# The last row group of the first norm turned by VectorE's block transposes and transfers within SBUF, in place of TensorE

## The chip, the core and the metric

One core of a Trainium2 chip runs the whole program. The core has a matrix engine (TensorE, PE in the profile; its weight loads are listed apart as PEld), three engines for elementwise work (VectorE or DVE, ScalarE or ACT, GpSimd or POOL), and SyncE (SP), which in this kernel issues nearly all transfers. Each engine works through its own queue in order; semaphores tie the queues together. Matmul results land in PSUM, eight banks of 128 × 512 words; everything else on the chip lies in SBUF (128 partitions) or in DRAM. The metric is the device time of one execution in microseconds, the median over runs.

## The reference, cut to what matters

```python
# x (1,2048,448); 16 heads of 28; mod = silu(c) @ w_mod gives six rows: sa, ca, ga, sb, cb, gb
h = _layernorm(x, axis=-1) * (1 + ca) + sa
qkv = h @ wqkv                       # split in q, k, v of 16 heads
p = softmax(q k^T * 28 ** -0.5)
x = x + ga * ((p v) @ wo)
h = _layernorm(x, axis=-1) * (1 + cb) + sb
x = x + gb * gmlp(h)                 # w_in, gelu, layernorm, w_sp over the rows, w_out
```

The change lies in the first line: the norm of the 2048 rows of x and what brings it into the layout in which the products of the next line take it, features on the partitions.

## The kernel before

**Tiles.** The rows come in NG = 4 groups of 512, each as four tiles of 128 rows (`xg`, `xn`). A group's normed rows have to stand as `hT[g]`: features on the partitions in four chunks (128, 128, 128 and 64 features; the last chunk's 64 are kept twice), 512 rows along the free axis. The products are done in three passes on operands split in a high part (fp32r) and a low part (what is left), so `hT[g]` has seven slots: the high parts of chunks 0 to 2, their low parts in slots 3 to 5, and slot 6 for chunk 3, high part in partitions 0 to 63 and low part in 64 to 127. `STEPS` lists the 11 pairs of slots that a product needs.

**Before the main part.** For a group g, `ln_stat` and `ln_rs` (VectorE and GpSimd) get mean and 1/sd of each row, `ln_norm` (VectorE) writes the normed rows `xn`, and `ln_transpose` (line 173) turns them: 16 transposes of 128 × 128 on TensorE into four PSUM banks `tp`, then per chunk one ScalarE activation that scales and shifts (`hfull`, by the columns ca and sa), one that writes the high part, and one VectorE subtraction for the low part. Line 372 copies 64 columns of `xn` so that the last chunk comes out twice. `ln_next(g)` (line 614) turns group g and, between the chunks, takes the statistics of group g + 1 and then norms it.

What uses `hT[g]` are `v_tile` (128 rows of V, 11 matmuls) and `qk_unit((m,), g)` (128 of the 896 Q and K columns for one group, 11 matmuls). In this text "unit (m, g)" is such a Q/K unit. Behind a unit ScalarE writes its high part into a tile `qh`, VectorE the low part into `ql`, and SP stores both to the DRAM scratch `qk_scr`. `qh` and `ql` have two buffers each, so the third unit in a row takes over the buffer of the first.

**Order.** It is written by hand (the scheduler is off): the loop at line 634 goes over g = 1, 2, 3 and lists v tiles, units (0, g) and (3, g), and pieces of the modulation: `mod_acc` (VectorE products of w_mod with silu(c)), `mod_split` (their high and low part), and `mod_bc` and `mod_col` (a sum over the partitions on TensorE, `pc`, read by VectorE; `mod_col` then sends a row through DRAM into a column, by SP). At g = 3 the early buffers are given up, the head buffers `kst` and `qst` take their place, are cleared (`pads`), and head 0 is loaded from `qk_scr`.

**The ramp.** Behind the loop the units left (line 970) run with the first maxima of the attention between their matmuls: `m_first` issues one product `mt` of 128 queries by 512 keys, and VectorE reduces it to its maximum (`pm`, line 717). Units take one of three PSUM banks there, maxima one of the four others. 80 maxima are done in the ramp, then the main part over 16 heads begins.

The second norm of the kernel already has a group turned in another way: `h2_turn` (line 1079) uses VectorE's transpose of 32 × 32 blocks, `h2_put` and `h2_load` move the blocks through DRAM, `h2_group` scales.

Of the kernel before, what the change touches and what calls it, by code (L numbers as in the profile page):

```python
# [8 lines left out]
F32 = mybir.dt.float32  # L9
F32R = mybir.dt.float32r  # L10
AF = mybir.ActivationFunctionType
# [9 lines left out]
NG = 4  # L21
# [78 lines left out]
def tile_adaln_mha_gmlp(ctx, tc, x, wqkv, wo, w_in, w_spT, b_sp, w_out, cT, w_mod0, w_mod, out):  # L100
# [122 lines left out]
    wv = e2.tile([128, 8, D], F32R, name="wv")  # L223
    ones_r = e2.tile([128, 128], F32R, name="ones_r")
    dve.memset(ones_r.bitcast(F32), 1.0)
    wms, xts, raws = {}, {}, {}


    banks, mode = list(range(7)), [None]
# [20 lines left out]

    def load_x(g, eng):
        xg = e1.tile([128, 4, D], F32, name="xg")
        for t0, t1 in ((0, 1), (1, 2), (2, 4)) if g == 0 else ((0, 4),):
            (act if t1 - t0 == 1 else eng).dma_start(xg[:, t0:t1, :], x[g, :, t0:t1])
        for t in range(4):
            xts[4 * g + t] = xg[:, t, :]
# [103 lines left out]
    def ln_norm(g, ts):  # L360
        mv, rs = mv1[g]
        for t in ts:
            xn = e1.tile([128, 512], F32, name="xn", bufs=4)
            dve.tensor_scalar(
                out=xn[:, :D],
                in0=xts.pop(4 * g + t),
                scalar1=mv[:, t, 0:1],
                scalar2=rs[:, t : t + 1],
                op0=ALU.subtract,
                op1=ALU.mult,  # L370
            )
            act.activation(xn[:, D:], xn[:, 384:D], AF.Copy)
            xn1.setdefault(g, []).append(xn)

    ln_stat(0, (0,))
# [233 lines left out]
    def ln_step(g, t):  # L609
        ln_stat(g, (t,))  # L610
        if t % 2:
            ln_rs(g, t - 1, t + 1)

    def ln_next(g):

        if g + 1 < NG:
            ln_transpose(
                xn1.pop(g), e1, hT[g], cols["ca"], cols["sa"], (act,) * 4, (dve,) * 4, None,
                lambda c: ln_step(g + 1, (0, 2, 1, 3).index(c)),
            )  # L620
            ln_norm(g + 1, range(4))
        else:
            ln_transpose(
                xn1.pop(g), e1, hT[g], cols["ca"], cols["sa"], (act,) * 4, (dve,) * 4, None, lambda c: c == 2 and mod_split(1, pool, e1, "wm", 4)
            )

    ln_next(1)
    load_x(3, sp)
# [5 lines left out]
    for g in range(1, NG):  # L634
        if g == 3:
            early.close()
            stk = att.enter_context(tc.tile_pool(name="stk", bufs=1))
            kq = [[stk.tile([128, S], F32R, name=f"{n}st{i}") for n in "kq"] for i in range(3)]
            kst, qst = [a[0] for a in kq], [a[1] for a in kq]
            npool = att.enter_context(tc.tile_pool(name="npool", bufs=2))  # L640
            late_s = ExitStack()
            late_l = late_s.enter_context(tc.tile_pool(name="late_l", bufs=2))

            def pads(i, eng):

                dve.memset(kst[i][64:128, :].bitcast(F32), 0.0)
                eng.memset(qst[i][64:128, :].bitcast(F32), 0.0)
                pool.memset(kst[i][64:86, :].bitcast(F32), 1.0)

            pads(0, dve)  # L650

            def load_head(h, c0=0, c1=S):
                k, q = kst[h % 3], qst[h % 3]
                if h > 2:
                    sp.dma_start(q[84:86, :].bitcast(F32), q[86:88, :].bitcast(F32))
                for r0, i in ((0, 0), (56, 1), (28, 0)):
                    sp.dma_start(k[r0 : r0 + 28, c0:c1].bitcast(F32), qk_scr[i][D + h * DH : D + (h + 1) * DH, c0:c1])
                for r0, i in ((0, 0), (28, 1), (56, 0)):
                    sp.dma_start(q[r0 : r0 + 28, c0:c1].bitcast(F32), qk_scr[i][h * DH : (h + 1) * DH, c0:c1])

            load_head(0, 0, 1536)
            for m in (0, 3):
                qk_unit((m,), g)
            load_head(0, 1536, S)
        v_tile(4 * g)
        if g == 3:
            mod_split(2, dve, late_l, "acc_l", 2)
        v_tile(4 * g + 1)
        if g == 3:
            pads(1, pool)  # L670
            pads(2, pool)
        if g + 1 < NG:
            ln_next(g + 1)
        for k in range(2):
            v_tile(4 * g + 2 + k)
            if g == 2 and k == 1:
                mod_bc("ga", 1, 0)
                mod_col("sb", 1, 1, 0.0)
            if g == 1 or g == 2 and k == 1:
                mod_acc(g, k if g == 1 else 0)  # L680
        if g < 3:
            for k, m in enumerate((0, 3)):
                qk_unit((m,), g)
                mod_acc(g, 3 - g + k)
            if g == 2:
                mod_acc(g, 3)
    mod_col("cb", 2, 0, 1.0)
    mod_bc("gb", 2, 1)
    late_s.close()
# [277 lines left out]
                    for fn, a in when.pop(e):  # L967
                        fn(*a)

    units = [(m, g) for m in (4, 1, 5, 2, 6) for g in range(NG) if g > 0 or m not in (1, 2)]  # L970
    for i, (m, g) in enumerate(units):
        qk_unit(
            (m,),
            g,
            {j: m_first for j in ((1, 3, 5, 7, 9) if i < 8 else (1, 4, 7, 10))},
            put_off=late.setdefault(2, []) if i == len(units) - 1 else None,
        )

# [701 lines left out]
```

## Time and profile before

| | us |
|---|---|
| median of 3 runs | 1370.16 (1369.8 to 1370.71) |
| the profiled execution | 1370.01 |
| its span, first to last instruction | 1368.2 |
| mean granted TensorE clock | 1.000 |

The profile is one execution, taken by the hardware profiler; times of its rows are counted from the start of the span. A timeline row gives start, length, engine, line and operation, what it writes and reads, how many instructions were merged, and in brackets how long the engine had been idle before it and what ended that. Rows of "SPq" are issues of transfers: the length is how long the issuing engine was taken, not how long the data moved. In 40 slices of the span TensorE stands at 9 of 10 or above in all but the last:

```profile
PE   9999999999999999999999999999999999999998
```

### The profile page before, as it was taken

How to read it: one execution, taken by the hardware profiler on the slowest of the kernel's cores; microseconds unless marked ns; L12 is line 12 of the kernel's file. 1: busy time of each engine (PE TensorE's matmuls, PEld its weight loads, DVE VectorE, ACT ScalarE, POOL GpSimd, SP SyncE). 2: the span in 40 equal slices, each digit the busy share in tenths (PEclk: the TensorE clock that was granted, in tenths of full speed). 3: DMA queues.
4: the chain of work that ended last, by engine and by line, in shares of the span. 5: the costliest groups of instructions: out<-in, count | busy, mean ns of one | idle time of the engine just before them, and what ended most of it. 6: DMA issues, size and time to landing. Idle time of an engine off the chain costs nothing.

```text
span 1368.2 us, 20793 instructions
## 1 busy us (share of the span) xinstructions
PE 1361.4 (100%) x7050; PEld 968.0 (71%) x7050; DVE 1112.8 (81%) x1764; ACT 805.2 (59%) x1475; POOL 361.8 (26%) x371
## 2 busy tenths in 40 slices
PE   9999999999999999999999999999999999999998
PEld 8888665556555555555565554788898888888898
DVE  7898899999999999999999991674467777999752
ACT  6623676777677667766776669555335545555411
POOL 2134434244535264654651002210021000000000
PEclk9999999999999999999999999999999999999999
DMA  8465756777677668777873110578604665787553
GB/s 292 135 173 181 234 151 214 210 219 217 222 200 233 189 215 250 215 220 224 248 217 98 43 44 23 181 222 265 228 31 154 221 201 179 254 291 258 180 163 111
DMA packets 144279, 260.21 MB, mean 190 GB/s; under 512 B 22120, under 2 KB 42986, under 8 KB 141626
## 3 DMA queue, kind: packets, MB, share of 16 engines
q1 hardware_dynamic: 141454, 254.69, 59.6%
q10 hardware_dynamic: 2718, 4.19, 0.8%
q8 instruction: 55, 0.90, 0.3%
q14 instruction: 52, 0.43, 0.1%
HBM read 177.67 MB, written 76.34 MB: 186 GB/s over the span
## 4 chain that ended last, share of the span: by engine, by line
PE 96%; issue 1%; DVE 1%; DMA 1%; POOL 0%; ACTq 0%; DVEq 0%; POOLq 0%; SPq 0%
PE st_ps L744 18%; PE mt L712 17%; PE o_ps L759 16%; PE z_ps L1429 5%; PE acc L1498 5%; PE acc L1497 5%; PE acc L1496 5%; PE z_ps L1199 5%; PE pq L407 5%; PE wo_ps L831 3%; PE pv L389 2%; PE y_ps L1569 2%; PE y_ps L1567 2%; PE y_ps L1568 2%; PE acc L1506 1%
## 5 line engine op out<-in xcount | busy, mean ns | idle before, releaser
L717 DVE TENSOR_REDUCE pm<-mt 128x1 f32<-128x512 f32 x1024 | 627.4, 678 | 8.0 <-PE mt L712 8.0
L748 ACT ACTIVATE P<-st_ps 128x512 f32<-128x512 f32 x1024 | 512.6, 640 | 203.1 <-PE st_ps L744 200.6
L744 PE MATMUL st_ps<-qst,kst 128*128 128x512 f32 x1024 | 409.3, 409 | 0.0
L712 PE MATMUL mt<-kst,qst 128*128 128x512 f32 x1024 | 401.5, 392 | 0.2 <-issue 0.2
L744 PEld LDWEIGHTS st_ps<-qst,kst 128*128 128x128 f32 x1024 | 191.3, 188 | 138.5 <-DVE pm L717 65.0
L759 PE MATMUL o_ps<-P,V 128*32 128x512 f32 x2048 | 240.0, 597 | 0.0
L712 PEld LDWEIGHTS mt<-kst,qst 128*128 128x128 f32 x1024 | 192.5, 188 | 34.8 <-ACT P L748 0.8
L869 POOL TENSOR_TENSOR ws_raw<-ws_raw 128x512 f32<-128x512 f32 x112 | 143.5, 1288 | 144.2 <-DMA ws_raw<-in_w_spT_dram 85.4
L1413 ACT ACTIVATE heapB<-raw_sp 128x512 fp32r<-128x512 f32 x156 | 96.7, 630 | 98.9 <-PE acc L1498 71.4
L759 PEld LDWEIGHTS o_ps<-P,V 128*32 128x32 f32 x2048 | 59.1, 109 | 127.2 <-issue 88.9
L1496 PE MATMUL acc<-heapB,heapA 128*128 128x512 f32 x312 | 121.4, 389 | 0.0
L1498 PE MATMUL acc<-heapB,heapA 128*128 128x512 f32 x312 | 121.4, 389 | 0.0
L765 DVE TENSOR_TENSOR osb<-osb,o_ps 128x512 f32<-128x512 f32 x82 | 56.3, 687 | 64.4 <-PE o_ps L759 62.9
L151 DVE TENSOR_TENSOR heapB<-raw_sp,heapB 128x512 fp32r<-128x512 f32 x112 | 74.5, 686 | 28.1 <-ACT heapB L1413 28.0
L1497 PE MATMUL acc<-heapB,heapA 128*128 128x512 f32 x222 | 86.5, 390 | 0.0
L1496 PEld LDWEIGHTS acc<-heapB,heapA 128*128 128x128 f32 x312 | 58.6, 188 | 12.1
L1498 PEld LDWEIGHTS acc<-heapB,heapA 128*128 128x128 f32 x312 | 58.6, 188 | 12.1
L407 PE MATMUL pq<-heapD,heapD 128*128 128x512 f32 x196 | 61.8, 390 | 0.0
L151 POOL TENSOR_TENSOR ws_raw<-ws_raw 128x512 fp32r<-128x512 f32 x44 | 56.7, 1289 | 3.5
L785 POOL TENSOR_TENSOR osb<-osb,rb 128x512 f32<-128x512 f32 x15 | 19.3, 1287 | 114.8 <-DMA rb<-r_scr 65.2
L1497 PEld LDWEIGHTS acc<-heapB,heapA 128*128 128x128 f32 x222 | 41.7, 188 | 9.0 <-DVE heapB L151 0.3
L1432 ACT ACTIVATE z<-z_ps 128x448 f32<-128x448 f32 x32 | 17.4, 545 | 48.0 <-PE z_ps L1429 48.0
(224 smaller groups left out, 1658.1 us busy)
## 6 DMA issues: line engine op xcount, KB each, us to landing
ws_raw<-in_w_spT_dram SPq DMA_DIRECT2D x136, 256.0 KB
ws_scr<-ws_raw SPq DMA_DIRECT2D x112, 256.0 KB
ws_raw<-ws_scr SPq DMA_DIRECT2D x88, 256.0 KB
raw_sp<-ws_scr SPq DMA_DIRECT2D x88, 256.0 KB
raw_sp<-in_w_spT_dram SPq DMA_DIRECT2D x68, 256.0 KB
wl_scr<-ws_raw SPq DMA_DIRECT2D x44, 256.0 KB
kst<-qk_scr SPq DMA_DIRECT2D x45, 224.0 KB
qst<-qk_scr SPq DMA_DIRECT2D x45, 224.0 KB
```

The lines of the kernel that those rows point to most:

```text
L151: eng.tensor_tensor(out=dst, in0=a, in1=hi.bitcast(F32), op=ALU.subtract)
L407: pe.matmul(pq, wqk[:, b, m * 128 : (m + 1) * 128], hT[g][:, a, :], start=j == 0, stop=j == NST - 1)
L712: pe.matmul(mt, qst[h % 3][:, t * 128 : (t + 1) * 128], kst[h % 3][:, kb * 512 : (kb + 1) * 512], start=True, stop=True)
L717: dve.tensor_reduce(out=pms[h][:, t, kb : kb + 1], in_=mt, axis=AX.X, op=ALU.max)
L744: pe.matmul(st, kst[h % 3][:, kt * 128 : (kt + 1) * 128], qst[h % 3][:, qb * 512 : (qb + 1) * 512], start=True, stop=True)
L748: act.activation(p, st, AF.Exp, scale=SCALE)
L759: pe.matmul(o[32 * qb : 32 * qb + 32, :], V[:, u % NT, h, :], ptiles.pop((u, qb)), start=u == a, stop=u == e - 1)
L869: pool.tensor_tensor(out=a, in0=a, in1=b, op=ALU.add if W_SUMS[v][2] > 0 else ALU.subtract)
L1413: act.activation(hi, raw[0], AF.Copy)
L1496: pe.matmul(o, zh[:, c], hi, start=p < 2 and kt == 0, stop=False, skip_group_check=p > 1)
L1497: pe.matmul(o, zh[:, c], lo, start=False, stop=False, skip_group_check=p > 1)
L1498: pe.matmul(o, zl[:, c], hi, start=False, stop=kt == 3, skip_group_check=p > 1)
```

## The change

Group 3 is no longer turned on TensorE. `load_x(3)` brings its rows in plain order, by four transfers in place of one, and `ln_next(2)`, which is called in the loop's turn for g = 1, goes on behind the norms of group 3: four block transposes on VectorE write back into the tile that x came in, sixteen transfers within SBUF put the blocks where the low parts of `hT[3]` belong, and a seventeenth repeats the 64 rows of the last chunk. A new function, `h_group`, then does what followed the transposes before, from SBUF where it had read PSUM: two ScalarE activations and a VectorE subtraction per chunk. It is called for chunks 0 and 2 behind unit (0, 2), and for 1 and 3 behind unit (3, 2). The turn for g = 2 has its pieces of the modulation in another order, and two units, (4, 0) and (4, 1), done there now and not in the ramp. Each of the ramp's 16 units has five maxima; before, the first eight had five and the other ten four.

```diff
     def load_x(g, eng):
         xg = e1.tile([128, 4, D], F32, name="xg")
-        for t0, t1 in ((0, 1), (1, 2), (2, 4)) if g == 0 else ((0, 4),):
+        if g == 3:
+            for t in range(4):
+                eng.dma_start(xg[:, t, :], x[g].rearrange("(a i) t d -> a t i d", a=4)[t])
+            turned.append(xg)
+        for t0, t1 in ((0, 1), (1, 2), (2, 4)) if g == 0 else ((0, 4),) if g < 3 else ():
             (act if t1 - t0 == 1 else eng).dma_start(xg[:, t0:t1, :], x[g, :, t0:t1])
...
-            act.activation(xn[:, D:], xn[:, 384:D], AF.Copy)
+            if g < 3:
+                act.activation(xn[:, D:], xn[:, 384:D], AF.Copy)
...
     def ln_next(g):
-        if g + 1 < NG:
-            ln_transpose(
-                xn1.pop(g), e1, hT[g], cols["ca"], cols["sa"], (act,) * 4, (dve,) * 4, None,
-                lambda c: ln_step(g + 1, (0, 2, 1, 3).index(c)),
-            )
-            ln_norm(g + 1, range(4))
-        else:
-            ln_transpose(
-                xn1.pop(g), e1, hT[g], cols["ca"], cols["sa"], (act,) * 4, (dve,) * 4, None, lambda c: c == 2 and mod_split(1, pool, e1, "wm", 4)
-            )
+        ln_transpose(
+            xn1.pop(g), e1, hT[g], cols["ca"], cols["sa"], (act,) * 4, (dve,) * 4, None,
+            lambda c: ln_step(g + 1, (0, 2, 1, 3).index(c)),
+        )
+        ln_norm(g + 1, range(4))
+        if g + 1 == 3:
+            block = turned[0].rearrange("p t d -> p (t d)").rearrange("p (b t i) -> p b t i", t=4, i=32)
+            for t, xn in enumerate(xn1.pop(3)):
+                dve.transpose(block[:, :, t, :], xn[:, :D])
+            lows = hT[3].bitcast(F32)
+            for r in range(4):
+                n = 4 if r < 2 else 3
+                for a in range(4):
+                    sp.dma_start(
+                        lows[32 * r : 32 * r + 32, 3 : 3 + n, a * 128 : (a + 1) * 128],
+                        block[32 * a : 32 * a + 32, r : r + 4 * n - 3 : 4].rearrange("p b t i -> p b (t i)"),
+                    )
+            sp.dma_start(lows[64:128, 6, :], lows[0:64, 6, :])
+
+    def h_group(g, cs):
+        for c in cs:
+            f, hi = e1.tile([128, 512], F32, name="hfull"), hT[g][:, c if c < 3 else 6, :]
+            src = hT[g][:, 3 + c, :].bitcast(F32)
+            act.activation(f, src, AF.Identity, scale=cols["ca"][:, c : c + 1], bias=cols["sa"][:, c : c + 1])
+            act.activation(hi, f, AF.Copy)
+            if c < 3:
+                sub(dve, hT[g][:, 3 + c, :], f, hi)
+            else:
+                sub(dve, hi[64:128], f[64:128], hi[64:128])
...
-        if g + 1 < NG:
+        if g < 2:
             ln_next(g + 1)
+        elif g == 2:
+            mod_split(1, pool, e1, "wm", 4)
         for k in range(2):
             v_tile(4 * g + 2 + k)
-            if g == 2 and k == 1:
-                mod_bc("ga", 1, 0)
-                mod_col("sb", 1, 1, 0.0)
-            if g == 1 or g == 2 and k == 1:
-                mod_acc(g, k if g == 1 else 0)
-        if g < 3:
+            if g == 1:
+                mod_acc(g, k)
+        if g == 1:
             for k, m in enumerate((0, 3)):
                 qk_unit((m,), g)
-                mod_acc(g, 3 - g + k)
-            if g == 2:
-                mod_acc(g, 3)
+                mod_acc(g, 2 + k)
+        elif g == 2:
+            for k, m in enumerate((0, 3)):
+                qk_unit((m,), g)
+                h_group(3, ((0, 2), (1, 3))[k])
+                if k == 0:
+                    mod_bc("ga", 1, 0)
+                    mod_col("sb", 1, 1, 0.0)
+                mod_acc(g, k)
+            for k in range(2):
+                qk_unit((4,), k)
+                mod_acc(g, 2 + k)
...
-    units = [(m, g) for m in (4, 1, 5, 2, 6) for g in range(NG) if g > 0 or m not in (1, 2)]
+    units = [(m, g) for m in (4, 1, 5, 2, 6) for g in range(NG) if g > {4: 1, 1: 0, 2: 0}.get(m, -1)]
     for i, (m, g) in enumerate(units):
         qk_unit(
             (m,),
             g,
-            {j: m_first for j in ((1, 3, 5, 7, 9) if i < 8 else (1, 4, 7, 10))},
+            {j: m_first for j in (1, 3, 5, 7, 9)},
```

How it moves the instructions is seen at two places. The first is SP's queue behind the loads of w_mod. Before, the stores of units (0, 1) (`qh_693`, `ql_694`) and (3, 1) come next, and then the row of the column sb:

```order
L243 DMA wm_558<-in_w_mod_dram 128x448
L426 DMA qk_scr0_65<-qh_693 128x512
L426 DMA qk_scr1_66<-ql_694 128x512
L426 DMA qk_scr0_65<-qh_712 128x512
L426 DMA qk_scr1_66<-ql_713 128x512
L341 DMA sb_scr_821<-row_820 1x448
```

With the change, the same place of SP's queue (`heapD1_93` holds `hT[3]`, `xg_506` the turned blocks; `qh_713` and `qh_732` are now units (0, 1) and (3, 1), `qh_812` is unit (0, 2)):

```order
L243 DMA wm_561<-in_w_mod_dram 128x448
L633 DMA heapD1_93<-xg_506 32x4x128 x8
L633 DMA heapD1_93<-xg_506 32x3x128 x8
L637 DMA heapD1_93<-heapD1_93 64x512
L431 DMA qk_scr0_65<-qh_713 128x512
L431 DMA qk_scr1_66<-ql_714 128x512
L431 DMA qk_scr0_65<-qh_732 128x512
L431 DMA qk_scr1_66<-ql_733 128x512
L431 DMA qk_scr0_65<-qh_812 128x512
L431 DMA qk_scr1_66<-ql_813 128x512
L345 DMA sb_scr_831<-row_830 1x448
```

Seventeen transfers have come in front of the four stores, and the stores of unit (0, 2) now stand ahead of the row of sb, where that row had been ahead of them.

The second place is ScalarE's queue in the turn for g = 2. Before, it scales group 3 out of the PSUM banks `tp` between the v tiles, and then takes the units (0, 2) (`qh_844`) and (3, 2):

```order
L393 ACTIVATE V_115<-pv_733 128x16x28
L187 ACTIVATE hfull_766<-tp_746,col_sa_87,col_ca_88 128x512
L194 ACTIVATE heapD1_93<-hfull_766 128x512
...
L187 ACTIVATE hfull_786<-tp_761,col_sa_87,col_ca_88 128x512
L194 ACTIVATE heapD1_93<-hfull_786 128x512
L393 ACTIVATE V_115<-pv_790 128x16x28
L393 ACTIVATE V_115<-pv_803 128x16x28
L420 ACTIVATE qh_844<-pq_832 128x512
L420 ACTIVATE qh_863<-pq_851 128x512
```

With the change (`qh_812` is unit (0, 2), `qh_854` (3, 2), `qh_881` (4, 0)):

```order
L398 ACTIVATE V_115<-pv_787 128x16x28
L425 ACTIVATE qh_812<-pq_800 128x512
L643 ACTIVATE hfull_818<-heapD1_93,col_sa_87,col_ca_88 128x512
L644 ACTIVATE heapD1_93<-hfull_818 128x512
L643 ACTIVATE hfull_822<-heapD1_93,col_sa_87,col_ca_88 128x512
L644 ACTIVATE heapD1_93<-hfull_822 128x512
L425 ACTIVATE qh_854<-pq_842 128x512
L643 ACTIVATE hfull_860<-heapD1_93,col_sa_87,col_ca_88 128x512
L644 ACTIVATE heapD1_93<-hfull_860 128x512
L643 ACTIVATE hfull_864<-heapD1_93,col_sa_87,col_ca_88 128x512
L644 ACTIVATE heapD1_93<-hfull_864 128x512
L425 ACTIVATE qh_881<-pq_869 128x512
```

All four scalings of group 3 have come behind the high part of unit (0, 2), and two of them behind that of (3, 2) as well.

2 lines of the change are left out of this document (1 added, 1 removed).

## The prediction

> **What bounds the kernel now.** I read the page first, then the timeline of each engine around the place of the change.
>
> ```profile
> span 1368.2 us, 20793 instructions
> PE 1361.4 (100%) x7050; PEld 968.0 (71%) x7050; DVE 1112.8 (81%) x1764; ACT 805.2 (59%) x1475; POOL 361.8 (26%) x371
> PE 96%; issue 1%; DVE 1%; DMA 1%; POOL 0%; ACTq 0%; DVEq 0%; POOLq 0%; SPq 0%
> ```
>
> TensorE (PE) is busy in 1361.4 of 1368.2 us and makes 96% of the chain that ended last. So a matmul taken away is worth its slot, and a wait put in front of PE costs its whole length: nothing later has slack to take it back. The profiled execution took 1370.01 us, 1.8 around its span; the median of the three runs, 1370.16, is 0.15 above it. Next, PE in the stretch that changes (start, length, count):
>
> ```profile
> 50.61 4.64 PE L389 MATMUL pv<-wv,heapD 128*128 128x448 f32 x22
> 55.10 1.91 PE L180 MATMUL tp<-ident,xn 128*128 128x128 f32 x16
> 56.76 4.74 PE L389 MATMUL pv<-wv,heapD 128*128 128x448 f32 x22
> ...
> 61.34 0.37 PE L332 MATMUL pc<-acc_h,ones_r 128*128 128x448 f32 x1
> ...
> 62.15 0.85 PE L407 MATMUL pq<-heapD,heapD 128*128 128x512 f32 x3
> ...
> 64.65 0.84 PE L407 MATMUL pq<-heapD,heapD 128*128 128x512 f32 x3
> ...
> 72.13 9.12 PE L389 MATMUL pv<-wv,heapD 128*128 128x448 f32 x44
> 81.09 0.37 PE L332 MATMUL pc<-acc_h,ones_r 128*128 128x448 f32 x1
> ...
> 81.91 0.39 PE L407 MATMUL pq<-heapD,heapD 128*128 128x512 f32 x1
> ...
> 85.28 0.39 PE L712 MATMUL mt<-kst,qst 128*128 128x512 f32 x1
> ```
>
> There is no gap: every row starts before the one ahead of it has ended. A Q/K unit takes 64.65 − 62.15 = 2.50 us, a pair of v tiles 55.10 − 50.61 = 4.49, the sums of pc 0.81.
>
> **What goes.** Group 3's 16 transposes on PE: 56.76 − 55.10 = **1.66 us**. The four 64-column copies on ScalarE (L372) go too, 0.26 us each on an engine that waited there. The two units m = 4 of groups 0 and 1 only move: 2.50 us each leave the ramp and stand ahead of group 3's first unit. The ramp still does 80 maxima (16 units by 5, before 8 by 5 and 10 by 4). Without waits PE would then be through (0,2) at 50.61 + 4.49 + 4.58 + 2.50 = 62.2 (four v tiles, then the unit); go through sums, (3,2), (4,0), (4,1) to 62.2 + 0.81 + 3 × 2.50 = 70.5; do (0,3), (3,3) and four v tiles to 84.5 and the sums to 85.3. The ramp would begin there instead of at 81.9 (two units later, 1.66 earlier), and its fifth maximum would be issued at 88.6 instead of 85.28.
>
> [...]
>
> **What comes on VectorE (DVE).**
>
> ```profile
> 50.07 0.94 DVE L364 TENSOR_SCALAR xn<-xg,mv,rs 128x448 f32<-128x448 f32 x2
> 51.18 0.93 DVE L364 TENSOR_SCALAR xn<-xg,mv,rs 128x448 f32<-128x448 f32 x2 [0.16 <-POOL rs L171]
> 52.03 0.68 DVE L307 TENSOR_SCALAR acc<-wm,silu 128x896 f32<-128x896 f32 x1
> ...
> 896.16 2.22 DVE L1086 STREAM_TRANSPOSE turn<-x 128x448 f32<-128x448 f32 x4
> ...
> 56.07 1.27 DVE L315 SCALAR_TENSOR_TENSOR acc<-wm,silu,acc 128x448 f32<-128x448 f32 x2
> ...
> 50.62 0.26 ACT L372 ACTIVATE xn<-xn 128x64 f32<-128x64 f32 x1 [2.62 <-DVE xn L364]
> ...
> 58.42 1.03 ACT L324 ACTIVATE acc_h<-acc 128x448 fp32r<-128x448 f32 x2
> ...
> 59.06 2.36 POOL L151 TENSOR_TENSOR acc_l<-acc,acc_h 128x448 fp32r<-128x448 f32 x2 [7.92 <-ACT acc_h L324]
> ```
>
> Four block transposes of this very shape stand in the second norm: 2.22 us. They follow the norms, so 52.0 to 54.3. The acc products behind them, done at 57.3 (56.07 + 1.27), slip by 2.2 us to 59.5; ScalarE's split of acc (1.03) then ends near 60.5 and POOL's low parts (1.2 us each) near 62.5, in time for the sums, which now come after (0,2). Hidden, with 0.2 us to spare.
>
> **What comes on SyncE (SP), and who queues behind it.** Sixteen transfers within SBUF and a seventeenth that repeats 64 rows wait for the transposes, so the first is issued at 54.3. The four stores of the units (0,1) and (3,1) are queued behind them; before, they went at once:
>
> ```profile
> 53.78 0.33 SPq L426 DMA_DIRECT2D qk_scr<-qh  x1
> ...
> 139.42 1.23 SPq L737 DMA_DIRECT2D qst<-nt  x2
> 192.10 0.65 SPq L771 DMA_DIRECT2D rt<-osb  x1
> 192.85 0.66 SPq L655 DMA_DIRECT2D qst<-qst  x1
> ...
> 398.89 6.14 SPq L796 DMA_DIRECT2D heapD<-osb  x8
> ...
> 898.41 3.01 SPq L1090 DMA_DIRECT2D hs_scr<-turn  x4
> ```
>
> This kernel's transfers from SBUF to SBUF occupy SP for 0.62 (1.23 / 2, pieces of 512 B as in the change), 0.65, 0.66 and 0.77 us (6.14 / 8); a store to DRAM for 0.33. Against that, four transfers with as many 512-byte pieces in all as the sixteen (1792) left SP in 3.01 us, though to DRAM. Bounds: 0.19 a transfer (that row spread over 16) and 0.85; I take **0.65**, by the first three rows. 17 × 0.65 = 11.05: SP is free for the store of (0,1) at 65.4.
>
> [...]
>
> **Who waits for that store.** qh has two buffers: ScalarE's qh for (0,2) overwrites that of (0,1), so it waits until the store has landed. How long that takes:
>
> ```profile
> 101.41 0.32 SPq L426 DMA_DIRECT2D qk_scr<-qh  x1
> ...
> 103.81 0.63 ACT L417 ACTIVATE qh<-qf 128x512 fp32r<-128x512 f32 x1 [0.38 <-DMA qk_scr<-qh]
> ```
>
> 2.4 us from issue to reader. So (0,2)'s qh starts at **T = 65.4 + 2.4 = 67.8**, where PE was done at 62.2. The scaling of group 3 is queued behind it on ScalarE:
>
> ```profile
> L1187 ACT ACTIVATE hfull<-heap,col_sb,col_cb x8: 803/804/807, 922.5 to 950.2; 128x512 f32<-128x512 f32 x8
> L1188 ACT ACTIVATE heap<-hfull x8: 632/632/633, 923.4 to 951.1; 128x512 fp32r<-128x512 f32 x8
> ...
> 64.85 0.60 ACT L420 ACTIVATE qh<-pq 128x512 fp32r<-128x512 f32 x1 [1.87 <-PE pq L407]
> ...
> 58.55 0.69 DVE L151 TENSOR_TENSOR heapD<-hfull,heapD 128x512 fp32r<-128x512 f32 x1 [0.60 <-ACT heapD L194]
> ...
> 66.09 1.14 DVE L309 SCALAR_TENSOR_TENSOR acc<-wm,silu,acc 128x896 f32<-128x896 f32 x1
> ```
>
> ScalarE: qh 0.60, chunks 0 and 2 at 0.80 + 0.63 each, qh of (3,2) 0.60, chunks 1 and 3: the last hi part at T + 7.1. DVE goes ql, low parts 0 and 2 (to T + 4.3), two pc readers, acc, ql (to T + 6.8), low parts 1 and 3: **T + 8.1 = 75.9**. Unit (0,3) needs chunk 3 at its tenth matmul, 70.5 + 9 × 0.227 = 72.5 (2.50 / 11 a matmul). First stop of PE: 3.3 us.
>
> **What is late next.** DVE goes on with two acc products and ql of (4,0), to T + 10.9. Then ql of (4,1) waits for its qh, whose buffer holds (3,2); that store stands behind the sb column on SP:
>
> ```profile
> 64.04 0.29 SPq L341 DMA_DIRECT2D sb_scr<-row  x1
> 65.18 1.61 SPq L344 DMA_DIRECT2D col_sb<-sb_scr  x3
> ...
> 69.76 1.28 DVE L315 SCALAR_TENSOR_TENSOR acc<-wm,silu,acc 128x448 f32<-128x448 f32 x2
> 71.53 1.76 DVE L646 MEMSET kst<- 64x2048 f32 x1 [0.49 <-DVE acc L315]
> ...
> 82.78 0.60 DVE L336 COPY bc_gb<-pc 128x448 f32<-128x448 f32 x1
> 83.31 3.08 DVE L717 TENSOR_REDUCE pm<-mt 128x1 f32<-128x512 f32 x5
> ```
>
> The row is ready at T + 5.5, the column takes SP 2.8 us (64.04 to 66.8), the store lands 2.4 later at T + 10.7, qh and ql end at T + 12.1, and the last acc pair at T + 13.3. From the end of that pair (71.04) to the first maximum (83.31) DVE works 12.27 us with no wait for PE: memsets, ql, acc low parts, pc readers. So the first maximum starts at T + 25.6 and frees its bank at T + 26.2 = **94.0**. Maxima have four banks, so the fifth is issued only then, 5.4 us after 88.6. The 3.3 us lie inside these 5.4. Behind that DVE needs 5 × 0.61 us a unit, PE 16 × 0.227 = 3.6, so the lag melts and nothing more is lost. Net: T + 26.2 − 88.6 − 1.66 = T − 64.1 = **+3.7 us**; 1370.0 + 3.7 = **1373.7**.
>
> **Rivals.**
> 1. *The queue is quick (the other side).* If the sixteen go at the price of L1090's pieces, SP is free near 58, T falls below 62.2, PE never stops and the 1.66 us remain: 1370.0 − 1.7 = 1368.4. It decides at T = 64.1, that is 0.435 us a transfer: below it the change gains, above it loses. For it: the row of 3.01 us, same pieces. Against: all four rows of SBUF-to-SBUF lie at 0.62 or more.
> 2. *Only the first stop counts.* If DVE's chain after chunk 3 is shorter than I make it (qh of (4,1) not held up, memsets early), the maxima are in time and the loss is 3.3 − 1.7 = 1.6: 1371.6. Against: the 12.27 us stretch was back to back before.
> 3. *The transposes are worth more than their slots*, because PE also loses time around them that the modelled ends hide: over 2.7 us gained, below 1367.3. [...]
>
> That the change doesn't do what it says is excluded by the order: 16 transposes fewer on PE, the same matmuls otherwise, the same 80 maxima ahead of the main part.
>
> **How the numbers follow.** Forecast 0.62 (slots of 0.53 to 0.85: +1.6 to +7.1, likeliest 1373.7), rival 1 0.22, rival 2 0.10, rival 3 0.06. About 0.2% (2.7 us) is what a measurement here can tell from no change. Of the forecast 0.50 lies above it and 0.12 below; so slower 0.50, same 0.12 + 0.22 + 0.10 = 0.44, faster 0.06. The range takes in the forecast and rivals 1 and 2: 1368.3 to 1377.1; the forecast's own is 1371.6 to 1377.1.
>
> **What would show it.** Right: SP's seventeen transfers end near 65; ScalarE's qh before the first scaling waits some 5 us for the DMA of qh; a hole of about 3 us in PE inside (0,3) and one of about 2 at the third to fifth maximum, with DVE's first maximum near 93. Rival 1: transfers over by 60, no hole in PE. Wrong altogether: a hole elsewhere, such as at the sums, whose cover is 0.2 us thin, or a main part whose length changed.

## The result and the profile after

The changed kernel takes 1379.14 us (median of 4 runs, 1377.70 to 1381.22), the kernel before 1370.43 (1369.80 to 1370.80, 4 runs): ratio 1.0066, 95% interval 1.0054 to 1.0078. It is 8.7 us slower; forecast were 3.7 us, with 1377.1 as the upper end of the range. The profiled execution took 1377.70 us. Three of the runs below (the turn alone, through DRAM, and own buffers with the products moved) have one execution of 1681 us or more; it counts in the median given, not in the ratio.

The lines of the page that answer to those shown of before: the span, the busy times, and the shares of the chain that ended last.

```profile
span 1375.8 us, 20778 instructions
PE 1363.1 (99%) x7034; PEld 966.7 (70%) x7034; DVE 1116.0 (81%) x1770; ACT 803.7 (58%) x1469; POOL 359.4 (26%) x369
PE 91%; DVE 3%; DMA 2%; issue 2%; ACT 1%; SPq 1%; POOL 1%; ACTq 0%; DVEq 0%; POOLq 0%
```

PE has sixteen transposes less to do and is busy 1.7 us longer; its share of the chain falls from 96% to 91%, and DVE, DMA and SP's queue come in: PE now waits for them. Where, its timeline shows (start, length; in brackets the idle time ahead and what ended it):

```profile
70.14 0.61 PE L412 MATMUL pq<-heapD,heapF 128*128 128x512 f32 x2
71.17 0.50 PE L412 MATMUL pq<-heapD,heapD 128*128 128x512 f32 x1 [0.42 <-ACT heapD L644]
72.54 0.73 PE L412 MATMUL pq<-heapD,heapD 128*128 128x512 f32 x2 [0.87 <-ACT heapD L644]
...
74.39 0.50 PE L412 MATMUL pq<-heapD,heapD 128*128 128x512 f32 x1 [0.42 <-ACT heapD L644]
...
76.11 0.50 PE L412 MATMUL pq<-heapD,heapD 128*128 128x512 f32 x1 [0.99 <-DVE heapD L151]
76.83 0.73 PE L412 MATMUL pq<-heapD,heapF 128*128 128x512 f32 x2 [0.22 <-DVE heapD L151]
...
79.91 9.12 PE L394 MATMUL pv<-wv,heapD 128*128 128x448 f32 x44
...
89.98 0.40 PE L412 MATMUL pq<-heapD,heapD 128*128 128x512 f32 x1
93.46 0.77 PE L743 MATMUL mt<-kst,qst 128*128 128x512 f32 x1 [3.08 <-DMA qst<-qk_scr]
...
97.68 0.40 PE L743 MATMUL mt<-kst,qst 128*128 128x512 f32 x1
```

Unit (4,1) ends its issue at 70.6 (70.14 and two slots of 0.23), where the forecast had 70.5. The two units of group 3 then take until 79.91: 9.3 us for 5.0 us of matmuls, a **first stop of 4.3 us**, in pieces, for ScalarE's and VectorE's parts of group 3. The sums lose 0.3 (79.91 + 8.96 for the v tiles + 0.81 is 89.7; the ramp begins at 89.98). Then comes a **second stop of 3.1 us** that the prediction did not have: the first maximum waits for the load of head 0's query. After it the matmuls are slow: from the first to the fifth maximum 97.68 − 93.46 = 4.22 us, before 85.28 − 82.45 = 2.83, so **1.4 us** more. Together 9.1 us; less the 1.66 of the transposes that is 7.4 of the 7.6 between the spans (1375.8 − 1368.2). So the rest of the kernel is as long as before, within 0.2.

SP's queue, ScalarE, and VectorE with GpSimd in the same stretch:

```profile
54.52 10.98 SPq L633 DMA_DIRECT2D heapD<-xg  x16
65.56 0.59 SPq L637 DMA_DIRECT2D heapD<-heapD  x1
66.25 0.52 SPq L431 DMA_DIRECT2D qk_scr<-qh  x1
...
82.92 4.95 SPq L680 DMA_DIRECT2D kst<-qk_scr  x3
87.92 1.23 SPq L682 DMA_DIRECT2D qst<-qk_scr  x3
```

```profile
69.16 0.60 ACT L425 ACTIVATE qh<-pq 128x512 fp32r<-128x512 f32 x1 [7.98 <-DMA qk_scr<-qh]
69.65 0.81 ACT L643 ACTIVATE hfull<-heapD,col_sa,col_ca 128x512 f32<-128x512 f32 x1
```

```profile
81.56 1.27 DVE L319 SCALAR_TENSOR_TENSOR acc<-wm,silu,acc 128x448 f32<-128x448 f32 x2
83.32 1.76 DVE L669 MEMSET kst<- 64x2048 f32 x1 [0.49 <-DVE acc L319]
85.29 1.81 POOL L671 MEMSET kst<- 22x2048 f32 x1 [23.19 <-ACT acc_h L328]
...
95.11 1.27 DVE L748 TENSOR_REDUCE pm<-mt 128x1 f32<-128x512 f32 x2
```

And what SP waited for between 80 and 93 us (us in total, times, longest):

```profile
SPq L680 <- POOL kst L671: 3.8, 1, 3.8
```

Read in order this is one chain: seventeen transfers hold SP until 66.15; the store of unit (0,1) follows, and ScalarE's qh of (0,2) has waited 7.98 us for it when it starts at T = 69.16; group 3's scaling is behind it (69.65); VectorE, which takes what ScalarE leaves it, clears head 0's key buffer at 83.32 (before at 71.53); GpSimd's ones, written into the same buffer, follow at 85.29 and end at 87.10; one of SP's three key loads waits for them (the 3.8 us), and the query loads behind it on SP go out at 87.92. PE is ready for the first maximum at 90.4 (89.98 + 0.39) and issues it at 93.46.

Windows over the same stretch (from:to, length, PE busy, granted clock, share of the DMA engines, GB/s) show why the maxima are slow:

```profile
92.80:93.00 0.20, 0.00 (x0) 1.00 1.08 410
93.00:93.20 0.20, 0.00 (x0) 0.61 1.02 348
96.20:96.40 0.20, 0.20 (x2) 0.50 0.00 0
96.40:96.60 0.20, 0.20 (x2) 0.86 0.36 51
```

The granted clock falls to one half at 93.04 (0.61 is 22% at full, 78% at half) and is back at 96.46: 3.41 us, of which PE worked 3.0. Before, it stays at 1.00 here. The four executions of the changed kernel have spans of 1375.8, 1377.3, 1377.3 and 1379.4 us at mean clocks of 0.999, 0.998, 0.998 and 0.995; a stretch of 3.41 us at half lowers the mean by 0.0012, so these are by estimate one, two, two and four stretches. The profiled execution is the one with the fewest, which would account for the median being 1 us further off than the profiles; the other three were not profiled. Nor need every such stretch come from a stop that the change makes: in five profiles of the experiments the mean granted clock of the first 50 us is 0.97 (four of them) or 0.93 (the turn alone), by estimate one stretch or two, and one of the five is that of the kernel before with an edit that acts only past 70 us.

### The profile page after: what moved, and what is told of

It is laid out like the page before. It is cut to its first block, busy times and chain, and to the rows that moved or that the text cites. A ratio compares the mean times of both kernels' runs of the same rounds, so it can differ in the third digit from the quotient of the medians.

```text
span 1375.8 us, 20778 instructions
## 1 busy us (share of the span) xinstructions
PE 1363.1 (99%) x7034; PEld 966.7 (70%) x7034; DVE 1116.0 (81%) x1770; ACT 803.7 (58%) x1469; POOL 359.4 (26%) x369
## 4 chain that ended last, share of the span: by engine, by line
PE 91%; DVE 3%; DMA 2%; issue 2%; ACT 1%; SPq 1%; POOL 1%; ACTq 0%; DVEq 0%; POOLq 0%
PE st_ps L775 18%; PE mt L743 17%; PE o_ps L790 16%; PE z_ps L1460 5%; PE acc L1529 5%; PE acc L1528 5%; PE acc L1527 5%; PE z_ps L1230 5%; PE pq L412 3%; PE wo_ps L862 3%; PE y_ps L1600 2%; PE y_ps L1598 2%; PE y_ps L1599 2%; PE acc L1537 1%; PE acc L1536 1%
```

## The experiments

Theory A is that chain. The rivals named in the expectations: B, group 3's transfers are late by themselves and the stores only stand in front of the same wait; C, the moved units cost; D, the slow matmuls have nothing to do with the stop; E, the 512-byte pieces are the price, not the number of transfers; F, the head's load is late for SP or the DMA engines and not for VectorE. Every run was timed beside the kernel before, at 1369.93 (the first four), 1370.32 (the next four), 1369.97 (the three after them) and 1370.38 us (the last).

**The two units moved, nothing else** (in the kernel before):

```
                 mod_acc(g, 3)
+                for k in range(2):
+                    qk_unit((4,), k)
...
-    units = [... if g > 0 or m not in (1, 2)]
+    units = [... if g > {4: 1, 1: 0, 2: 0}.get(m, -1)]
-            {j: m_first for j in ((1, 3, 5, 7, 9) if i < 8 else (1, 4, 7, 10))},
+            {j: m_first for j in (1, 3, 5, 7, 9)},
```

> The kernel before, with only the two Q/K units (4,0) and (4,1) moved ahead of group 3's units; group 3 keeps its transposes on TensorE. Theory A (everything lost comes from group 3's data being late, through the queue of SP): nothing is late here, so no stop of TensorE before the first maximum and the time of before, 1370.4 within 0.7 us. Rival C (the move itself costs, because VectorE gets the two units' low parts ahead of the memsets that the first head's load waits for): a stop at the first maximum as in the changed kernel, 2 us or more on top, 1372.5 or above.

Measured: 1370.27 us, ratio 1.0002 (0.9993 to 1.0011), no wait of PE between 60 and 110 us. The move is free; rival C falls.

**The turn alone**: the changed kernel with that edit undone.

```
             for k in range(2):
-                qk_unit((4,), k)
                 mod_acc(g, 2 + k)
...
-    units = [... if g > {4: 1, 1: 0, 2: 0}.get(m, -1)]
+    units = [... if g > 0 or m not in (1, 2)]
-            {j: m_first for j in (1, 3, 5, 7, 9)},
+            {j: m_first for j in ((1, 3, 5, 7, 9) if i < 8 else (1, 4, 7, 10))},
```

> The changed kernel with the two units put back in the ramp. Theory A: group 3 is ready at the same moments as in the changed kernel (last low part near 76.8), so TensorE, which gets to unit (0,3) at 65.6 instead of 70.6, is through (3,3) at 79.9 as there: the stop in these units grows by 5.0 us and the ramp does 5.0 us more. VectorE has two low parts and one wait less, so its memsets start 2.5 us sooner (80.8), the first maximum is issued near 90.9 instead of 93.5 and with no stretch at half clock: 3.9 us back. In all 1.1 us over the changed kernel, about 1380 us. Rival C (the two units only cost, they cover nothing): the loss of the changed kernel shrinks to the first stop, about 1375 us. If the move covered its full 5.0 us and nothing came back: 1384 us.

Measured: 1379.83 us (1379.41 without the one execution of 1681.65), 1.0068 (1.0056 to 1.0081): 0.3 to 0.7 us over the changed kernel. So 5.0 us of cover in front of group 3 buy almost nothing. As A had it, without them the first maximum is issued (at 94.29) with no wait for the load of head 0: what they hide at the first stop comes back at the second. The sizes are less sure, since this profile ran 2.2 us late from its start (first v tile at 52.98, in the changed kernel 50.78) and at half clock from 70.1 to 83.8 (below).

**TensorE kept busy in the second stop**:

```
+            for _ in range(again - 1 if j == 0 else 0):
+                pe.matmul(pqs[0], ..., start=True, stop=True)
...
+            again=15 if i == 0 else 1,
```

> The changed kernel with the ramp's first matmul issued 14 times more, 3.2 us of work that overwrites itself, in the stop ahead of the first maximum. Theory A: the half clock behind that stop comes from the stop itself; with TensorE busy the maxima are issued at full speed and the granted clock shows 1.0 throughout. The first maximum still starts at 93.4, the fifth at 96.3 instead of 97.7: 1.4 us faster than the profile of the changed kernel, 1.4 to 3 us in the median (its other executions show a lower mean clock), 1376 to 1377.7. Rival D (the slow matmuls are slow for another reason, such as the load of the next head or VectorE's maxima): durations of 0.63 us stay, and the time stays at 1379.1.

Measured: 1377.79 us, 1.0052 (1.0039 to 1.0064), 1.35 us under the changed kernel, the median 0.1 above the range expected. PE's timeline and a window of this run:

```profile
90.57 3.38 PE L412 MATMUL pq<-heapD,heapD 128*128 128x512 f32 x14
...
94.16 0.47 PE L745 MATMUL mt<-kst,qst 128*128 128x512 f32 x1
...
96.98 0.39 PE L745 MATMUL mt<-kst,qst 128*128 128x512 f32 x1
```

```profile
73.00:76.40 3.40, 3.28 (x7) 0.51 0.02 6
94.00:98.00 4.00, 4.00 (x18) 1.00 0.54 167
```

With PE busy the first to the fifth maximum take 2.82 us again, at full clock: the slow matmuls came from the stop, and D falls. In this execution the clock fell in the first stop instead, where the changed kernel's profile had kept it.

**Buffers of their own for (0,2) and (3,2)**, so that ScalarE need not wait for the stores:

```
+            own = not mid and g == 2
-            hi = stage.tile([128, 512], F32R, name="qh")
+            hi = e1.tile([128, 512], F32R, name="qh_own") if own else stage.tile(...)
-            lo = stage2.tile([128, 512], F32R, name="ql")
+            lo = e1.tile([128, 512], F32R, name="ql_own") if own else stage2.tile(...)
```

> The changed kernel with qh and ql of the units (0,2) and (3,2) in buffers of their own, so that they don't wait for the stores of (0,1) and (3,1). The seventeen transfers stay. Theory A, as forecast (the stores queued behind the transfers hold up ScalarE, and group 3's scaling behind it): ScalarE's qh of (0,2) runs at 62.2 with no wait, the scaling starts when the transfers have landed, near 67.6 instead of 69.65; VectorE also loses its wait at (4,1), so the memsets start near 80.4 instead of 83.3 and the first maximum near 90.5: 3 to 4.5 us faster than the changed kernel, 1374.6 to 1376. Rival B (the transfers' own way is what is late, and the stores only stand in front of the same wait): the scaling still starts at 69 or later, and less than 1 us comes back, 1378 or above.

Measured: 1374.39 us, 1.0030 (1.0019 to 1.0042), 4.75 us under the changed kernel. ScalarE and PE:

```profile
67.62 0.82 ACT L644 ACTIVATE hfull<-heapD,col_sa,col_ca 128x512 f32<-128x512 f32 x1 [4.57 <-DMA heapD<-xg]
```

```profile
89.83 0.47 PE L744 MATMUL mt<-kst,qst 128*128 128x512 f32 x1 [1.77 <-DMA qst<-qk_scr]
```

The scaling starts at 67.62 (expected 67.6) and now waits for the transfers themselves; the first maximum comes 3.6 us sooner, and no stretch at half clock follows it (mean granted clock 1.00 from 50 to 100 us). The first stop is 2.3 us where it was 4.3, the second 1.8 where it was 3.1; with the 1.4 of the slow maxima this makes up the 4.6 us between the two profiles. B is right only on what remains: the stores cost 2.0 us at the scaling, the transfers' own way the rest.

**Five more transfers**: the seventeenth issued six times.

```
-            sp.dma_start(lows[64:128, 6, :], lows[0:64, 6, :])
+            for _ in range(6):
+                sp.dma_start(lows[64:128, 6, :], lows[0:64, 6, :])
```

> The changed kernel with its seventeenth transfer issued five times more (the same rows written again). Theory A: each takes about 0.6 to 0.7 us of SP, the stores and everything behind them come 3.0 to 3.5 us later, and TensorE loses as much: 1382 to 1383.5, up to 2 us more with a longer stretch at half clock. Rival B (the queue isn't what holds group 3): less than 1 us more than the changed kernel, up to 1380.

Measured: 1389.29 us, 1.0133 (1.0118 to 1.0149). The dose was larger than meant, 1.95 us of SP for each of the six where the single one of the changed kernel took 0.59; each repeat writes the rows of the one ahead, and that it waits for it is an inference:

```profile
67.24 11.72 SPq L638 DMA_DIRECT2D heapD<-heapD  x6
```

```profile
81.96 0.60 ACT L425 ACTIVATE qh<-pq 128x512 fp32r<-128x512 f32 x1 [19.76 <-DMA qk_scr<-qh]
```

T is 12.8 us later than in the changed kernel (81.96 − 69.16), and the span 12.5 longer (1388.3 − 1375.8); in both, 1.0 is a late start of this execution (first v tile at 51.77, there 50.78). The medians lie 10.2 apart. What holds SP here reaches the end nearly whole, as a sum: the first stop grew by more than that, with the half clock behind it (below), and the second shrank to 1.0 us, with the maxima behind it at full pace (2.83 us from the first, at 106.14, to the fifth, at 108.97).

**Through DRAM**: four stores of the same 512-byte pieces and five loads for the seventeen transfers, the Q/K stores between them.

```
-            for r in range(4):
...
+            for a in range(4):
+                sp.dma_start(turn_scr.rearrange("(b j) n -> j b n", j=32)[..., a * 128 : (a + 1) * 128],
+                             block[32 * a : 32 * a + 32].rearrange("p b t i -> p b (t i)"))
+    def turn_load():
+        for c in (0, 2, 1):
+            sp.dma_start(lows[:, 3 + c, :], turn_scr[c * 128 : (c + 1) * 128, :])
+        for r in (0, 64):
+            sp.dma_start(lows[r : r + 64, 6, :], turn_scr[384:D, :])
...
         elif g == 2:
+            turn_load()
```

> The changed kernel with the transposed blocks sent through DRAM: four stores of the same 512-byte pieces, then the stores of (0,1) and (3,1), then five loads, in place of the seventeen transfers. Theory A: the price is per transfer and not per piece, so the four occupy SP for about 3 us (54.5 to 57.5), the Q/K stores follow at once, ScalarE's qh of (0,2) runs at 62.2 with no wait for a DMA, and the scaling starts near 64.2, 5.4 us sooner than in the changed kernel and in time for unit (0,3). The first maximum stops TensorE for 0.7 us at most: 1369 to 1370, and faster than the variant with buffers of its own. Rival E (the pieces of 512 bytes are what takes the time, so that two passes through DRAM are no quicker): the four stores take 8 us or more, the scaling starts at 69 or later, 1378 or above.

Measured: 1376.42 us, 1.0040 (1.0026 to 1.0054): 2.7 us back where 9 to 10 were expected. SP and ScalarE:

```profile
55.98 3.02 SPq L632 DMA_DIRECT2D turn_scr<-xg  x4
59.10 1.21 SPq L432 DMA_DIRECT2D qk_scr<-qh  x1
60.40 1.55 SPq L432 DMA_DIRECT2D qk_scr<-ql  x1
```

```profile
67.64 0.81 ACT L648 ACTIVATE hfull<-heapD,col_sa,col_ca 128x512 f32<-128x512 f32 x1 [3.10 <-DMA heapD<-turn_scr]
```

Neither theory holds whole. 1792 pieces leave SP in 3.02 us in four stores (0.76 each) and in 10.98 in sixteen transfers (0.69 each), so the price is per transfer, against E; that the four went to DRAM and the sixteen within SBUF is a difference that no run takes apart. But the Q/K stores behind them then took 1.21 and 1.55 us of SP instead of 0.3 to 0.5, and the loads landed only at 67.6. This profile ran 1.5 us late from its start (block transposes at 53.72, in the changed kernel 52.26), so the scaling comes 3.5 us sooner after the transposes, where 5.4 were expected. The second stop stays, 3.2 us with half clock behind it (0.50 from 92.6 to 95.8 us).

**The products and the sb column moved**, the transfers as in the change (`mod_col_put`, split off from `mod_col`, sends the column's row through DRAM):

```
         elif g == 2:
+            for k in range(4):
+                mod_acc(g, k)
             for k, m in enumerate((0, 3)):
...
-                    mod_col("sb", 1, 1, 0.0)
-                mod_acc(g, k)
+                    mod_col("sb", 1, 1, 0.0, True)
             for k in range(2):
                 qk_unit((4,), k)
-                mod_acc(g, 2 + k)
+            mod_col_put("sb")
```

> The changed kernel with the four products of the modulation (4.2 us of VectorE) put ahead of unit (0,2), in VectorE's idle stretch of 10.6 us, and the sb column's four transfers on SP behind the stores of (3,2), (4,0) and (4,1). The seventeen transfers stay. Theory A: the first stop (4.3 us in the units of group 3) stays; VectorE's memsets start near 79.2 instead of 83.3, the load of the first head lands near 89.4 to 90, before TensorE gets to the first maximum; the second stop (3.1 us) and the half clock behind it go: 4 to 4.6 us faster than the changed kernel, 1374.5 to 1375.5. Rival F (the load of the first head is late by SP's queue or the DMA engines, not by VectorE's memsets): the first maximum still starts at 92 or later, less than 2 us come back.

Measured: 1374.74 us, 1.0030 (1.0019 to 1.0042), 4.4 us under the changed kernel. VectorE and PE:

```profile
79.36 1.76 DVE L677 MEMSET kst<- 64x2048 f32 x1 [0.48 <-DVE ql L151]
```

```profile
91.53 0.47 PE L752 MATMUL mt<-kst,qst 128*128 128x512 f32 x1 [1.04 <-POOL qst L678]
```

The memset starts at 79.36 (expected 79.2), the second stop shrinks from 3.1 to 1.0 us, and the maxima run at full clock (1.00 from 90 to 104 us). Nothing ahead of the memset got quicker: the sixteen transfers took 11.82 us here (10.98 in the changed kernel), the scaling started at 70.42 (69.65), and the first stop was 4.8 us (4.3), part of it at half clock (0.50 from 73.2 to 76.2 us). So F falls as the main cause. What is left of the second stop comes at least in part from the edit itself: the sb column now stands right ahead of head 0's loads on SP, which waits 2.2 us for the column's row to land, so the key loads go out at 83.48, after the ones are done (83.12). The row above names GpSimd's clearing of head 1's query buffer as what ended the wait; this product does not read that buffer, so the name is not evidence.

**The last two together** (the products moved, and through DRAM), both diffs as above:

> Both: through DRAM, and the products and the sb column moved as in the last run. Theory A: no stop of TensorE is left, and the sixteen transposes stay saved: 1370.2 less 1.7, 1368.5 us (1368.2 to 1369.2), faster than the kernel before. If the transposes on TensorE were worth nothing, 1370.2.

Measured: 1371.64 us, 1.0005 (0.9996 to 1.0014), 2.4 us above the range expected. SP and ScalarE:

```profile
61.80 1.93 SPq L648 DMA_DIRECT2D heapD<-turn_scr  x3
```

```profile
67.79 0.81 ACT L656 ACTIVATE hfull<-heapD,col_sa,col_ca 128x512 f32<-128x512 f32 x1 [4.66 <-DMA heapD<-turn_scr]
```

The second stop is gone (the first maximum is issued at 89.31 without a wait); the first is not (3.7 us, half clock included), since the scaling has to wait for the loads until 67.8.

**The loads first**, and buffers of their own besides, on top of that: the five loads directly behind their four stores, ahead of the stores of (0,1) and (3,1).

```
                 sp.dma_start(turn_scr..., block[...])
+            for c in (0, 2, 1):
+                sp.dma_start(lows[:, 3 + c, :], turn_scr[c * 128 : (c + 1) * 128, :])
+            for r in (0, 64):
+                sp.dma_start(lows[r : r + 64, 6, :], turn_scr[384:D, :])
...
-            turn_load()
```

> The variant through DRAM with the products moved, and besides: the five loads of group 3 directly behind its four stores on SP, ahead of the stores of (0,1) and (3,1), with qh and ql of (0,2) and (3,2) in buffers of their own so that ScalarE doesn't wait for those. In the variant before it the loads stood behind four stores of 256 KB with the DMA engines busy throughout, and landed at 67.8. Theory A: the loads are issued at about 60 to 63 and landed by 65, so group 3 is ready for unit (0,3) at 70.6, TensorE has no stop, the transposes' 1.7 us are gained: 1368.5 to 1369.3 us, faster than the kernel before. Rival E (the way through DRAM with 512-byte pieces can't land before 67 in any order): a stop in (0,3) with its stretch at half clock as in the variant before it, 1371 to 1372.

Measured: 1369.03 us, 0.9993 (0.9985 to 1.0002). SP, ScalarE and a window of PE:

```profile
62.38 1.29 SPq L647 DMA_DIRECT2D heapD<-turn_scr  x3
```

```profile
65.02 0.82 ACT L655 ACTIVATE hfull<-heapD,col_sa,col_ca 128x512 f32<-128x512 f32 x1 [0.57 <-DMA heapD<-turn_scr]
```

```profile
70.00:90.00 20.00, 20.00 (x94) 1.00 0.71 210
```

PE has no idle time left in the stretch. From the first load's issue to the scaling are 2.6 us (62.38 to 65.02), in the run before 6.0 (61.80 to 67.79): the loads had been late through the megabyte of Q/K stores that they stood behind. The order and the buffers were not tried apart. The median is 0.9 us below the kernel before, the interval just includes no change. This profile's span is 1368.6, with its block transposes 1.4 us later than in the changed kernel's (53.66 against 52.26) after a stretch at reduced clock in the first 50 us (mean 0.97 there).

**Own buffers and the products moved, with the seventeen transfers**, both diffs as above:

> The changed kernel with its seventeen transfers, and both edits that keep the lateness from spreading: own buffers for qh and ql of (0,2) and (3,2), and the products and the sb column moved. Theory A (each cuts its own part of one chain): the scaling starts at 67.6, the stop in (0,3) is 1.5 us as in the variant with own buffers, the stop at the first maximum is gone as in the variant with the products moved; what is left of the loss and the 1.7 us gained cancel: 1370 to 1371.5. If the two edits save the same microseconds and not different ones, 1374.5.

Measured: 1372.40 us, 1.0017 (1.0008 to 1.0026), 2.0 and 2.3 us under each edit alone, and 0.9 above the range expected. PE:

```profile
88.64 0.47 PE L753 MATMUL mt<-kst,qst 128*128 128x512 f32 x1 [1.24 <-DMA qst<-qk_scr]
```

A first stop of 2.0 us and this second one of 1.2 were left; less the 1.7 gained they make up the 1.6 us by which the span exceeds that of before (1369.8 to 1368.2). Apart, the edits save 4.75 and 4.40 us, together 6.74: 2.4 of these microseconds they share, the rest is different. They cut overlapping parts of one chain, and not all of it; the sb column stands ahead of the head's loads here too, and SP waits 2.1 us for its row.

**The transposes twice** (the kernel before, group 3):

```
-            for t in range(4):
+            for t in [*range(4)] * (2 if dsts is hT[3] else 1):
                 pe.transpose(...)
```

> The kernel before with the sixteen transposes of group 3 issued twice (into the same places): what they are worth on TensorE. As forecast, their slots: 1.66 us more than the kernel before, 1372.0 (1371.7 to 1372.4). [...] If other work of TensorE hid them: 1370.3.

Measured: 1371.71 us, 1.0021 (1.0008 to 1.0034): 1.74 us more. PE's timeline of this run:

```profile
55.24 3.65 PE L180 MATMUL tp<-ident,xn 128*128 128x128 f32 x32
58.65 4.74 PE L389 MATMUL pv<-wv,heapD 128*128 128x448 f32 x22
```

32 transposes take 3.41 us where 16 took 1.66: their slots, no more.

**VectorE late and nothing else** (the kernel before):

```
-                dve.memset(kst[i][64:128, :].bitcast(F32), 0.0)
+                for _ in range(3 if i == 0 else 1):
+                    dve.memset(kst[i][64:128, :].bitcast(F32), 0.0)
```

> The kernel before, with VectorE's first memset of head 0's key buffer issued three times, so that VectorE alone is late by 4.28 us (2 x 2.14, the distance of two memsets in the trace) and nothing else is. What the prediction followed (VectorE's lag reaches TensorE only through the maxima): the first maximum is issued at 82.45 without a wait, the fifth waits for VectorE's first, which ends at 83.3 + 4.3 + 0.6 = 88.2 instead of 85.28: 2.9 us more, 1373.0. What the profile of the changed kernel suggests (the load of head 0 stands behind these memsets, and it is the tighter of the two): the first maximum waits for the load of qst until 76.16 + 4.3 + 5.5 = 86.0, the fifth follows at 88.8 at full clock: 3.5 us more, up to 5 with a stretch at half clock, 1373.8 to 1375.3, and the trace names the DMA of qst ahead of the first maximum.

Measured: 1376.67 us, 1.0050 (1.0036 to 1.0064). PE's timeline:

```profile
87.40 0.76 PE L713 MATMUL mt<-kst,qst 128*128 128x512 f32 x1 [2.95 <-DMA qst<-qk_scr]
...
91.73 0.39 PE L713 MATMUL mt<-kst,qst 128*128 128x512 f32 x1
```

The kernel before, made late on VectorE alone, shows the second stop of the changed kernel: the same 3 us, the same DMA of qst, the same slow maxima (4.33 us from the first to the fifth). This execution ran 1.36 us late from its start (its first v tile at 51.97, before 50.61), so the first maximum stands at 86.04 for the 86.0 expected. The time lies 1.4 us above the range given; in the profile the late start accounts for it, a stretch at reduced clock in the first 50 us (mean 0.97 there) that has nothing to do with the edit, and for the other four executions, at mean clocks of 0.996 to 0.998, it is open.

## Why the prediction was wrong, step by step

The direction and the way were right: the transposes leave, SP's queue becomes the wait, ScalarE's qh passes it to group 3, VectorE passes it to the ramp. The size was not.

| step | forecast | measured |
|---|---|---|
| transposes' slots | 1.66 | 1.74 (issued twice) |
| sums hidden behind (0,2), 0.2 to spare | no stop | no stop at 62.3 |
| SP free for the store of (0,1) | 65.4 | 66.25 |
| store to reader | 2.4 | 2.91 |
| T, qh of (0,2) | 67.8 | 69.16 |
| first stop | 3.3 | 4.3 |
| VectorE's first maximum | T + 25.6 | T + 25.95 (95.11) |
| fifth maximum issued | 94.0 | 97.68 |

Two terms were too small. *The queue*: 0.65 a transfer was near (10.98 / 16 = 0.69), but the first went out 0.2 later, and the store landed 0.5 later than in the row of before that gave the 2.4: T is 1.4 us late, and so is all behind it. In the other profiles with these sixteen they took 10.84 to 11.82 us, 0.68 to 0.74 each.

*The step that failed* is "What is late next". It followed VectorE's lag to the maxima it has to take, and to nothing else that VectorE releases. The memsets were in its sum of 12.27 us as work; that the load of head 0 waits for one of them, on SP and through GpSimd, was not. The sign stood in the profile of before, between the rows that the sum used:

```profile
SPq L657 <- POOL kst L648: 3.1, 1, 3.1
```

In the kernel before the loads of qst went out at 76.16, and the 5.5 us that they take to the first maximum in the changed kernel (87.92 to 93.46) put them there at about 81.7 by estimate, 0.8 ahead of the 82.45 at which they were needed, while VectorE's first maximum was done at 83.9, 1.4 ahead of the fifth at 85.28: the path through the load had less slack than the one that the forecast took. By VectorE alone the fifth maximum would have come at T + 26.2 = 95.4; it came 2.3 us later: 0.9 by the load (93.46 and 2.83 at full clock make 96.3) and 1.4 by the half clock behind the stop, a loss that the sum put at nothing and that no row of before showed. 1.4 and 2.3 are 3.7 of the 4.0 us that the profiled execution lies above the forecast (1377.7 against 1373.7). Without the half clock it would have come to 1376.3, inside the forecast's range: the late queue and the load alone did not carry it out. The median is 1.4 higher again; more stretches at half clock in the other executions would account for it, but this is argued from their mean clocks.

The rivals: *the queue is quick* fell at 0.69 us a transfer, well above its 0.435, and the row of L1090 that spoke for it was the price of four transfers: 3.01 us there, 3.02 in the run through DRAM. *Only the first stop counts* fell: the second, 3.1 us and 1.4 of slow maxima, cost as much as the first with its 4.3. *The transposes are worth more than their slots* fell with the run that doubles them (1.74 us more for sixteen).

## What to carry to other kernels

In these rows a transfer's price on the queue that issues it went by the transfer (0.69 us with 96 to 128 pieces, 0.76 with 448), and the bill was paid by whoever was queued behind it: before work is moved from a bound engine to transfers, follow the next few entries of that queue to their readers. When an engine off the critical path becomes late, follow everything it releases, its memsets and the loads that wait for them too, and compare their slacks; the shortest one decides. Look in the profile of before at what the queues wait for, too. A bound TensorE that is made to stop can lose more than the stop: here 1.4 us on top of 3.1.

## What the runs showed of the hardware

Not expected was that stops cost clock, and in the profiles read closely by multiples of one length. The edges of the reduced stretches in two more profiles, read from windows as above, the first that of the run with five more transfers, the second that of the turn alone:

```profile
74.00:74.20 0.20, 0.00 (x0) 0.61 0.00 0
94.40:94.60 0.20, 0.20 (x2) 0.69 1.26 338
```

```profile
70.00:70.20 0.20, 0.00 (x0) 0.76 0.99 379
83.60:83.80 0.20, 0.20 (x1) 0.61 1.05 215
```

From 74.04 to 94.52 are 20.48 us, and in the run of the turn alone from 70.10 to 83.76 are 13.66: six and four times the 3.41 us of the changed kernel. In four more profiles (TensorE kept busy, through DRAM, the products moved, the last two together) the one stretch between 70 and 100 us is 3.4 us long, from 73.05 to 76.46 in the first of them. What sets that length no run shows. In the changed kernel TensorE had been idle for 2.7 us (90.38 to 93.04) when the clock fell. Which stop triggers it could not be told from its length: 1.77 us in one piece did not (own buffers), while 0.39, 0.40 and 0.47 us with matmuls between them did in the profile of the products moved and through DRAM, where the clock falls to 0.50 at 74.85, and 0.28, 0.40 and 0.46 in the same place did not (own buffers and the products moved, mean clock of the execution 1.000). That the same stop costs differently from one execution to the next would fit this and the four executions of the changed kernel, with mean clocks of 0.995 to 0.999, but only one of the four was profiled, so it stays an inference.

The other: behind much work a queue's entries themselves can get long. Stores of 256 KB that occupy SP for 0.32 to 0.53 us in most rows took 1.21 and 1.55 us behind the 1792 small pieces, in both runs that have the Q/K stores right behind them (through DRAM, and with the products moved besides). What sets the length was not tried.
